# One order of VectorE's bit operations in the joint slots, and the start of eight weight conversions, changed in an attention and two-layer feed-forward kernel

## The chip, the cores and the metric

The kernel runs on one core of a Trainium2 chip. The metric is the device time of one execution in microseconds; the kernel before takes 620.14 us (median of 3 runs, 619.54 to 620.14).

Five engines work side by side and wait for each other by semaphores: TensorE (PE in the rows, with its weight loads as PEld), VectorE (DVE), ScalarE (ACT), GpSimd (POOL) and SyncE (SP), which only issues transfers here. Each runs its instructions in the order in which the program gave them.

## The reference

Attention over 2 x 8 heads of 768 positions and 64 channels with 8 global and 96 local positions, then two feed-forward layers on the 1536 x 512 result. All in float32; the weights arrive as float64 words.

```python
a = softmax(where(keep, scale * q @ k.T + bias, -1e9))
x = (a @ v).transpose(0, 2, 1, 3).reshape(1536, 512)
h = x @ moe_w_in                                  # 512 -> 2048
x = (maximum(h, 0) + alpha * minimum(h, 0)) @ moe_w_out
h = x @ moe2_w_in
g = P(h) / (Q(h) + 1e-6)                          # a rational function
return g @ moe2_w_out
```

## The kernel before, in words

**Tiling.** The attention goes by blocks of 128 queries; a pair of steps (two pairs of heads) is one `u`, from 0 to 23. The first layer of the feed-forward part goes by groups of 512 tokens and chunks of 128 hidden channels; one group and one chunk is one step. A step is a first product (line 859: 12 matmuls of 128 x 512 into one bank), the alpha unit on its result, and a second product (line 930: 12 matmuls). Every float32 operand of a product is split into a high half, rounded to the format in which TensorE reads, and a low half, the rest.

**Stages.** `u` 0 to 9 run alone (up to 42 us). Then come 16 joint slots, `joint_slot(s, halves)` (line 969), `s` 0 to 15, each of which runs `u = 10 + s` of the attention and step `s` of the first layer in one hand-written order. All later steps run in `plain_slot` (line 1004).

**One joint slot.** `opening(u)` (716): TensorE computes the scores of `u`, and in odd `u` the value products of two earlier `u`; VectorE takes the reciprocals of `u - 1` (563), after which GpSimd normalises (556), and adds the bias to the scores and takes the extreme (537, 4 instructions); ScalarE takes the exponentials (544, 4 instructions); in odd `u` ScalarE and VectorE store the two halves of a finished block (`xhi` 614, `xlo` 615). Then `first(s)`. `leaky(s)` (862) issues ScalarE's `act` (866) and VectorE's `h` (867); what it returns issues ScalarE's `ghi` (870), and what that returns VectorE's `glo` (871). `glo` is the last reader of bank 3, into which `first(s + 1)` writes. `turning(u)` (742): TensorE transposes the probabilities of `u - 1` (574, 576) into banks 0 and 1, where the bias instructions of `u` have read, and one block of raw keys (odd `u`) or queries (even `u`) into bank 2 (460); ScalarE copies the probabilities out (582) and takes the high halves of keys (475) or queries (489); the functions for the low halves (`klo` 479, `qlo` 490) are returned as `lows` for VectorE. `second(s - 1)` comes last.

**Weight conversions.** Half a chunk of weights (512 KB of float64 words) is one job. `tick` (353) is called twice in a slot, with numbers `2s - 1` and `2s`, and moves each started job on by one stage:

- at its start: ScalarE scales one word of the pair into one of two `de` buffers (397);
- one tick later: three VectorE bit operations that assemble the float32 (386, 387, 388; 386 and 387 read `de`, each reads the one before) and a call of `load_more` are put into the list `join`, from which `join_step(n)` issues up to `n`; the next load goes into the staging buffer that 388 has read;
- one tick later: the high half on ScalarE (372 where it is `held`, else 374), preceded by whatever is left in `join`;
- one tick later: the low half on VectorE (377).

Where a job starts at each tick there are two sets of bit operations in a slot: those of the job started at `2s - 3` (the older; issued whole inside the tick `2s - 1`) and those of the job started at `2s - 2` (the younger; issued by the `join_step` calls of `joint_slot`). The high half of the older is `held` until behind `ghi`; that of the younger, and the next scale, come with the tick `2s`.

**The plan.** `plan_weights` (253) gives each job the tick of its start. With `CH` = 8 and `KEPT` = 12, the jobs of the first eight chunks start at ticks up to 11; those of chunks 8 to 11, whose halves are written to DRAM (`spill`, 241) and read back later (`reload`, 246), at 10, 12, ..., 24; those of chunks 12 to 15 from 31 on. Transfers are issued by SyncE in program order.

Of the kernel before, what the change touches and what calls it, by code (L numbers as in the profile page):

```python
# [49 lines left out]
CH = NF // 2  # L50
KEPT = CH + 4
# [14 lines left out]
class Kernel:  # L66
# [186 lines left out]
    def plan_weights(self):  # L253
        self.steps = [(0, 0, fc, fc % NEARLY) for fc in range(CH)]
        self.steps += [(0, 1, fc, fc % NEARLY) for fc in (*range(NEARLY, CH), *range(NEARLY))]
        self.steps += [(0, 2, fc, fc) for fc in range(NF)]
        self.steps += [(0, g, fc, fc) for g in (0, 1) for fc in range(CH, NF)]
        self.steps += [(1, g, j, j) for g in (2, 0) for j in range(CH)]
        self.steps += [(1, 1, j, j) for j in range(NF)]
        self.steps += [(1, g, j, j) for g in (2, 0) for j in range(CH, NF)]  # L260
        runs = [s[:2] for s in self.steps]
        self.begins = {n for n in range(len(runs)) if n == 0 or runs[n - 1] != runs[n]}
        self.ends = {n - 1 for n in self.begins if n} | {len(runs) - 1}
        self.saves = {n for n in self.ends if runs[n] in runs[n + 1 :]}
        self.adds = {n for n in self.ends - self.saves if runs[n] in SAVED}
        jobs = {}
        for fc in range(CH):
            jobs[2 * fc - 6 if fc > 2 else 4 * fc - 17] = 0, fc, "in", fc % NEARLY
            jobs[2 * fc - 3 if fc else -5] = 0, fc, "out", fc % NEARLY
        half, layer = NGR * CH, NGR * NF  # L270
        spare = [(fc, kind) for fc in range(CH, NF) for kind in ("in", "out")]
        for t, (fc, kind) in enumerate(spare):
            jobs[10 + 2 * t if fc < KEPT else 15 + 2 * t] = 0, fc, kind, None if fc < KEPT else fc
        todo = []
        for n, free in ((0, LATE), (CH, layer - CH)):
            for k in range(CH):
                for kind, lag in (("in", 0), ("out", 5)):
                    todo.append((n + k, 2 * (free + k) + lag, kind))
        times = [t for t in range(48, 96) if (t % 2 == 0 or t in (55, 71) or t > 82) and t not in (64, 66, 80, 82, 85, 88, 91, 94, 95)]
        times += (107, 112, 117, 121, 125, *range(137, 160, 4))  # L280
        for t in times:
            ready = [x for x in todo if x[1] <= t]
            if ready:
                j, _, kind = job = min(ready)
                todo.remove(job)
                jobs[t] = 1, j, kind, j
        assert not todo
        self.starts = set(jobs)
        self.plan = [jobs[t] for t in sorted(jobs)]
# [555 lines left out]
    def moe(self):  # L845
# [6 lines left out]
        def first(n):  # L852
            m, g, fc, slot = steps[n]
            w = self.slots[slot]
            bk = banks[3 if n < LATE else n % 3]
            seq = [(a, b, c) for a, b in (("hi", "hi"), ("lo", "hi"), ("hi", "lo")) for c in range(NC)]
            for e, (a, b, c) in enumerate(seq):
                x = (self.xhi if b == "hi" else self.xlo)[g]
                nc.tensor.matmul(bk, w["in", a][:, c, :], x[:, c, :], start=e == 0, stop=e == len(seq) - 1)  # L859
            hbank[n] = bk  # L860

        def leaky(n):
            fc, h = steps[n][2], hbank.pop(n)
            t, hi, lo = self.act[n % 2], self.ghi[n % 2], self.glo[n % 2]
            sg, sa = self.sg[:, fc : fc + 1], self.sa[:, fc : fc + 1]
            nc.scalar.activation(t, h, AF.Copy, scale=sa)  # L866
            nc.vector.scalar_tensor_tensor(h, h, sg, t, ALU.mult, ALU.max)  # L867

            def halves():
                nc.scalar.activation(hi, h, AF.Copy, scale=sg)  # L870
                return lambda: nc.vector.scalar_tensor_tensor(lo, h, sg, hi.bitcast(F32), ALU.mult, ALU.subtract)  # L871

            return halves
# [43 lines left out]
        def second(n, parts=range(3)):  # L917
            m, g, fc, slot = steps[n]
            ys.add(n)
            w = self.slots[slot]  # L920
            hi, lo = self.ghi[n % 2], self.glo[n % 2]
            y = banks[4:8]
            begin, last = n in self.begins, n in self.ends
            wt = w["out", "hi"].rearrange("p c f -> p (c f)"), w["out", "lo"].rearrange("p c f -> p (c f)")
            order = [(d, e) for e in parts for d in range(4)]
            for d, e in sorted(order) if last else order:
                cols = slice(d * P, (d + 1) * P)
                a, b = ((hi, wt[0]), (hi, wt[1]), (lo, wt[0]))[e]
                lhs, rhs = (b[:, cols], a) if m == 0 else (a[:, cols], b)
                nc.tensor.matmul(y[d], lhs, rhs, start=begin and e == 0, stop=last and e == 2)  # L930
            if not last or 2 not in parts:
                return
            for d in range(4):
                if m == 0 or n == N - 1 or d < 3:
                    drain(n, d)
                else:
                    drains.append((n, d))
# [31 lines left out]
        def joint_slot(s, halves):  # L969
            u = JOIN // 2 + s  # L970
            opening, turning = halves or (lambda u: None, lambda u: ())
            if s >= CH + 2 and s < CH + 2 + NEARLY:
                self.reload(s - CH - 2)
            opening(u)
            held = []
            if s == 0:
                self.creep()
            else:
                while self.creeps:
                    self.creep()  # L980
                self.tick(True, 2 * s - 1 in self.starts, spread=True, held=held)
                self.join_step(2)
            first(s)
            halves = leaky(s)
            self.join_step(2)
            if s == 0:
                self.creep()
            lows = turning(u)
            low = halves()
            for high in held:  # L990
                high()
            for more in lows:
                more()
            low()
            if s == 0:
                self.creep()
            self.tick(True, 2 * s in self.starts, spread=True)
            if s:
                second(s - 1)
            if s == LATE - 1:  # L1000
                self.tick(True, 2 * s + 1 in self.starts)
                self.spill()
# [72 lines left out]
        def run(halves):  # L1075
            first_call = state["slot"] == 0
            if first_call:
                for s in range(LATE):
                    joint_slot(s, halves)
                state["slot"] = LATE  # L1080
                return
            self.moe_constants()
            for fc in range(NEARLY, CH):
                self.reload(fc)
            for s in range(LATE, N + 2):
                plain_slot(s)
# [41 lines left out]
```

## Time and profile before

| what | us |
|---|---|
| median of 3 runs | 620.14 (619.54 to 620.14) |
| the profiled execution | 619.92 |
| its span in the profile | 618.1 |
| TensorE busy, matmuls | 606.3 (98%) |
| VectorE busy | 498.4 (81%) |
| ScalarE busy | 404.7 (65%) |
| GpSimd busy | 130.8 (21%) |
| TensorE in the chain that ended last | 91% of the span |

The granted clock of TensorE is 0.9 or more of full speed in every one of the 40 slices of the page but the last. The joint slots lie between 42 and 174 us. In rows of instructions the columns are: start in us, duration in us, engine, line, operation, out<-in by the program's names, shapes and count; in square brackets the engine's idle time just before, and what ended it. Durations overlap a little with the next instruction on the same engine, so the step from one start to the next is the better price in a busy queue.

### The profile page before, as it was taken

Reading aid. Unit: us, or ns where it says so; the run is one execution under the profiler, and the core shown is the slowest. Engines: PE = TensorE matmul, PEld = TensorE weight load, DVE = VectorE, ACT = ScalarE, POOL = GpSimd, SP = SyncE. Lnnn points to the kernel's source line nnn. Section 1 sums busy time; section 2 is a strip of 40 time slices with the busy share of each in tenths; the row PEclk is TensorE's granted clock in tenths of the full one; section 3 lists DMA queues with packets and bytes.
Section 4 is the critical chain, followed back from the end, with each engine's and each line's share of the span. In section 5 each row is a group of like instructions: output and inputs, shape, how many; then the busy total and the mean of one; then the engine's idle time right before and its main releaser. Section 6 shows DMA issues by size and latency. Waiting matters only on the chain.

```text
span 618.1 us, 9432 instructions
## 1 busy us (share of the span) xinstructions
PE 606.3 (98%) x3187; PEld 499.1 (81%) x3187; DVE 498.4 (81%) x960; ACT 404.7 (65%) x826; POOL 130.8 (21%) x202
## 2 busy tenths in 40 slices
PE   8999999999999999999999999999999999999996
PEld 6688878888888888888888888888888888888884
DVE  6988899776457768668579889999899977788976
ACT  6997777876455444354354587787877766766772
POOL 6863223322100000000000012122222222222221
PEclk9999999999999999999999999999999999999998
DMA  9999999878889534315322401211201000400302
GB/s 211 252 277 272 284 291 299 289 261 271 251 275 353 169 97 116 95 35 150 123 68 70 135 1 34 89 47 37 101 1 35 0 1 0 137 1 1 136 1 74
DMA packets 81426, 82.53 MB, mean 134 GB/s; under 512 B 41994, under 2 KB 58394, under 8 KB 81370
## 3 DMA queue, kind: packets, MB, share of 16 engines
q1 hardware_dynamic: 81190, 81.58, 44.3%
q8 instruction: 27, 0.44, 0.3%
q14 instruction: 29, 0.24, 0.1%
q10 hardware_dynamic: 180, 0.27, 0.1%
HBM read 59.94 MB, written 19.92 MB: 129 GB/s over the span
## 4 chain that ended last, share of the span: by engine, by line
PE 91%; DVE 5%; ACT 2%; issue 1%; POOL 0%; DVEq 0%; ACTq 0%
PE bank L859 41%; PE bank L930 41%; PE bank L518 2%; PE bank L595 2%; PE bank L574 1%; PE bank L597 1%; ACT prob L544 1%; PE bank L576 1%; PE bank L460 1%; DVE prob L537 1%; DVE dx L388 1%; PE bank L201 1%; DVE dx L387 0%; DVE dx L386 0%; DVE glo L871 0%
## 5 line engine op out<-in xcount | busy, mean ns | idle before, releaser
L915 POOL TENSOR_TENSOR glo<-act,ghi 128x512 fp32r<-128x512 f32 (+1 forms) x49 | 62.4, 1274 | 382.8 <-ACT ghi L911 362.7
L859 PE MATMUL bank<-xhi,winhi_f 128*128 128x512 f32 x256 | 68.4, 389 | 0.0
L859 PE MATMUL bank<-xhi,winlo_f 128*128 128x512 f32 x256 | 68.4, 389 | 0.0
L859 PE MATMUL bank<-xlo,winhi_f 128*128 128x512 f32 x256 | 68.4, 389 | 0.0
L556 POOL TENSOR_SCALAR prob<-prob,rec 128x232 f32<-128x232 f32 (+1 forms) x96 | 48.8, 526 | 70.0 <-DVE rec L563 43.5
L867 DVE SCALAR_TENSOR_TENSOR bank<-bank,sg,act 128x512 f32<-128x512 f32 x48 | 36.3, 757 | 31.4 <-ACT act L866 31.3
L870 ACT ACTIVATE ghi<-bank,sg 128x512 fp32r<-128x512 f32 x48 | 33.3, 694 | 39.4 <-DVE bank L867 25.3
L866 ACT ACTIVATE act<-bank,sa 128x512 f32<-128x512 f32 x48 | 32.8, 683 | 37.6 <-PE bank L859 37.5
L859 PEld LDWEIGHTS bank<-xhi,winlo_f 128*128 128x128 f32 x256 | 48.0, 188 | 10.0
L859 PEld LDWEIGHTS bank<-xhi,winhi_f 128*128 128x128 f32 x256 | 48.0, 188 | 10.0
L859 PEld LDWEIGHTS bank<-xlo,winhi_f 128*128 128x128 f32 x256 | 48.0, 188 | 10.0
L544 ACT ACTIVATE prob<-prob,stat 128x232 f32<-128x232 f32 (+1 forms) x96 | 44.7, 470 | 14.9 <-DVE stat L537 12.8
L871 DVE SCALAR_TENSOR_TENSOR glo<-bank,sg,ghi 128x512 fp32r<-128x512 f32 x48 | 35.9, 747 | 18.8 <-PE bank L930 14.3
L882 ACT ACTIVATE stage<-bank 128x512 f32<-128x512 f32 (+1 forms) x49 | 28.8, 588 | 32.8 <-PE bank L859 32.8
L891 DVE SCALAR_TENSOR_TENSOR stage<-stage,abs_b 128x512 f32<-128x512 f32 (+1 forms) x49 | 36.1, 737 | 14.9 <-ACT stage L883 14.8
L397 ACT ACTIVATE de<-stage 128x512 f32<-128x512 f32 x59 | 39.5, 675 | 6.9 <-issue 3.2
L387 DVE SCALAR_TENSOR_TENSOR dx<-de,dx 128x512 int32<-128x512 int32 x59 | 40.9, 694 | 2.0
L388 DVE SCALAR_TENSOR_TENSOR dx<-stage,dx 128x512 int32<-128x512 int32 x59 | 40.9, 693 | 1.6
L911 ACT CAST ghi<-act 128x512 fp32r<-128x512 f32 (+1 forms) x49 | 30.2, 617 | 17.6 <-DVE act L908 15.2
L930 PE MATMUL bank<-wouthi_f,glo 128*128 128x512 f32 x144 | 41.1, 391 | 0.0
L930 PE MATMUL bank<-wouthi_f,ghi 128*128 128x512 f32 x144 | 40.9, 389 | 0.0
L930 PE MATMUL bank<-woutlo_f,ghi 128*128 128x512 f32 x144 | 40.9, 389 | 0.0
(240 smaller groups left out, 1418.4 us busy)
## 6 DMA issues: line engine op xcount, KB each, us to landing
stage<-in_moe_w_in_dram SPq DMA_DIRECT2D x32, 512.0 KB
stage<-in_moe_w_out_dram SPq DMA_DIRECT2D x32, 512.0 KB
part<-saved_f SPq DMA_DIRECT2D x16, 256.0 KB
saved_f<-part SPq DMA_DIRECT2D x12, 256.0 KB
out_dram<-part SPq DMA_DIRECT2D x11, 256.0 KB
rawk<-in_k_dram SPq DMA_DIRECT2D x10, 256.0 KB
rawq<-in_q_dram SPq DMA_DIRECT2D x10, 256.0 KB
va<-in_v_dram SPq DMA_DIRECT2D x10, 240.0 KB
```

Source lines behind the costliest of these rows:

```text
L387: lambda: nc.vector.scalar_tensor_tensor(y, e, -(2**31), y, ALU.bitwise_and, ALU.bitwise_or),
L388: lambda: nc.vector.scalar_tensor_tensor(y, low, 29, y, ALU.logical_shift_right, ALU.bitwise_or),
L397: nc.scalar.mul(self.de[n % 2], self.staged(n)[:, :, :, 1].bitcast(F32), 2.0**-112)
L544: nc.scalar.activation(p[:, j - e, :w], p[:, j - e, :w], AF.Exp, bias=st[:, j : j + 1], scale=-1.0, accum_out=st[:, 4 + j : 5 + j],)
L556: nc.gpsimd.tensor_scalar(p[:, j, :w], p[:, j, :w], r[:, e + j : e + j + 1], 1.0, ALU.mult, ALU.mult)
L859: nc.tensor.matmul(bk, w["in", a][:, c, :], x[:, c, :], start=e == 0, stop=e == len(seq) - 1)
L867: nc.vector.scalar_tensor_tensor(h, h, sg, t, ALU.mult, ALU.max)
L870: nc.scalar.activation(hi, h, AF.Copy, scale=sg)
L871: return lambda: nc.vector.scalar_tensor_tensor(lo, h, sg, hi.bitcast(F32), ALU.mult, ALU.subtract)
L891: nc.vector.scalar_tensor_tensor(w, w, self.ab[:, 0:1], ab, ALU.add, ALU.mult)
L915: nc.gpsimd.tensor_tensor(lo, u, hi.bitcast(F32), ALU.subtract)
L930: nc.tensor.matmul(y[d], lhs, rhs, start=begin and e == 0, stop=last and e == 2)
```

## The change

In `plan_weights`, the starts of the jobs of chunks 8 to 11 move four ticks on: 14, 16, ..., 28 instead of 10, 12, ..., 24. In `joint_slot`, slots 1 to 5 (`two`) issue no bit operation of the younger set ahead of `first` and `leaky`. In odd `u`, one of them follows `h`, then come `glo`, then `klo`, and `join_step(4)` issues the other two and `load_more`. In even `u` none follows `h`; `qlo` and `glo` come in the old order, then all three. In the other slots two bit operations still stand ahead of `h`; in odd `u` the third follows `h`, and `glo` comes ahead of `klo`; in even `u` the third follows `glo`.

```diff
         for t, (fc, kind) in enumerate(spare):
-            jobs[10 + 2 * t if fc < KEPT else 15 + 2 * t] = 0, fc, kind, None if fc < KEPT else fc
+            jobs[14 + 2 * t if fc < KEPT else 15 + 2 * t] = 0, fc, kind, None if fc < KEPT else fc
...
             opening(u)
             held = []
+            two = 0 < s < CH - 2
             if s == 0:
                 self.creep()
             else:
                 while self.creeps:
                     self.creep()
                 self.tick(True, 2 * s - 1 in self.starts, spread=True, held=held)
-                self.join_step(2)
+                self.join_step(0 if two else 2)
             first(s)
             halves = leaky(s)
-            self.join_step(2)
+            if u % 2:
+                self.join_step(1 if two else 2)
             if s == 0:
                 self.creep()
             lows = turning(u)
             low = halves()
             for high in held:
                 high()
-            for more in lows:
+            for more in (low, *lows) if u % 2 else (*lows, low):
                 more()
-            low()
+            self.join_step(4)
             if s == 0:
                 self.creep()
             self.tick(True, 2 * s in self.starts, spread=True)
```

## Rows read from the trace of the kernel before

**Rows 1.** Busy time by stretch: us, then each engine; clock, DMA share, GB/s.

```profile
67.20:92.50 25.30, 23.90 (x154) 19.22 (x152) 23.55 (x55) 19.44 (x51) 6.74 (x13) 1.00 0.99 283
...
110.00:176.00 66.00, 65.99 (x460) 54.48 (x459) 41.66 (x108) 41.32 (x103) 15.65 (x36) 1.00 0.86 276
```

**Rows 2.** Instructions in order of time, TensorE, slots 6 and 7.

```profile
92.51 1.19 PE L859 MATMUL bank<-xhi,winhi__120 128*128 128x512 f32 x4 [1.09 <-DVE glo L871]
...
96.19 0.60 PE L460 MATMUL bank<-part,rawq 128*128 128x128 f32 x4
...
102.11 1.19 PE L859 MATMUL bank<-xhi,winhi__124 128*128 128x512 f32 x4
```

**Rows 3.** Instructions in order of time, VectorE, slot 3.

```profile
67.95 0.69 DVE L615 TENSOR_TENSOR xlo<-bank,xhi 128x512 fp32r<-128x512 f32 x1 [1.48 <-ACT xhi L614]
...
69.61 0.69 DVE L387 SCALAR_TENSOR_TENSOR dx<-de,dx 128x512 int32<-128x512 int32 x1
70.34 0.69 DVE L388 SCALAR_TENSOR_TENSOR dx<-stage,dx 128x512 int32<-128x512 int32 x1
70.94 0.42 DVE L386 TENSOR_SCALAR dx<-de 128x512 int32<-128x512 int32 x1
71.40 0.69 DVE L387 SCALAR_TENSOR_TENSOR dx<-de,dx 128x512 int32<-128x512 int32 x1
72.01 0.75 DVE L867 SCALAR_TENSOR_TENSOR bank<-bank,sg,act 128x512 f32<-128x512 f32 x1
72.67 0.68 DVE L388 SCALAR_TENSOR_TENSOR dx<-stage,dx 128x512 int32<-128x512 int32 x1
73.27 0.75 DVE L479 TENSOR_TENSOR klo<-bank,khi 128x480 fp32r<-128x480 f32 x2
73.93 0.74 DVE L871 SCALAR_TENSOR_TENSOR glo<-bank,sg,ghi 128x512 fp32r<-128x512 f32 x1
74.59 0.69 DVE L377 TENSOR_TENSOR woutlo__127<-dx,wouthi__126 128x512 fp32r<-128x512 f32 x1
75.19 0.17 DVE L563 RECIPROCAL rec<-rec 128x4 f32<-128x4 f32 x1
```

**Rows 4.** The same for ScalarE, slot 3.

```profile
70.38 0.71 ACT L397 ACTIVATE de<-stage 128x512 f32<-128x512 f32 x1 [1.69 <-issue]
71.00 0.67 ACT L866 ACTIVATE act<-bank,sa 128x512 f32<-128x512 f32 x1
...
72.80 0.69 ACT L870 ACTIVATE ghi<-bank,sg 128x512 fp32r<-128x512 f32 x1
```

**Rows 5.** The same for VectorE, slot 2 and its ends.

```profile
57.72 0.29 DVE L537 CUSTOM_DVE_ANT_0 prob<-bank,part 128x128 f32<-128x128 f32 x1 [1.17 <-PE bank L518]
...
59.63 0.69 DVE L387 SCALAR_TENSOR_TENSOR dx<-de,dx 128x512 int32<-128x512 int32 x1
...
65.14 0.17 DVE L563 RECIPROCAL rec<-rec 128x4 f32<-128x4 f32 x1
```

**Rows 6.** The same for ScalarE, slot 2.

```profile
61.00 0.67 ACT L866 ACTIVATE act<-bank,sa 128x512 f32<-128x512 f32 x1
...
62.43 0.61 ACT L489 ACTIVATE qhi<-bank 128x512 fp32r<-128x512 f32 x1
```

**Rows 7.** The same for VectorE, the reciprocal at the start of slot 6.

```profile
92.96 0.17 DVE L563 RECIPROCAL rec<-rec 128x4 f32<-128x4 f32 x1
```

**Rows 8.** The same for GpSimd, the normalisations of slots 5 and 6.

```profile
83.94 1.76 POOL L556 TENSOR_SCALAR prob<-prob,rec 128x232 f32<-128x232 f32 x4 [4.05 <-DVE rec L563]
...
93.31 2.44 POOL L556 TENSOR_SCALAR prob<-prob,rec 128x232 f32<-128x232 f32 x4 [6.24 <-PE bank L859]
```

**Rows 9.** The chain that ended last, in order of time, a piece in the plain slots.

```profile
193.03 2.72 PE bank L859 x12
```

**Rows 10.** Instructions in order of time, VectorE, slot 4.

```profile
78.32 0.87 DVE L388 SCALAR_TENSOR_TENSOR dx<-stage,dx 128x512 int32<-128x512 int32 x1
```

**Rows 11.** The same for GpSimd, slot 4.

```profile
78.59 0.97 POOL L501 CAST klo<-klo 128x384 fp32r<-128x384 f32 x1
```

## What the trace gave reason to expect

> **What bounds the kernel now.** I read the stages first: busy time by stretch shows TensorE with 65.99 of 66.00 us from 110 to 176, and the plain slots behind that are as full; the only hole of any size after 42 us is 1.40 us of idle TensorE between 67.2 and 92.5, where VectorE is busy 23.55 of 25.30 us [rows 1]. So whatever TensorE loses in the joint slots is never won back, and whatever it gains there arrives whole at the end. Then the rows of TensorE: 1.09 us of the hole stand before one matmul, the first of slot 6, and their releaser is `glo` (line 871) on VectorE [rows 2]. Then VectorE instruction by instruction in slot 3 [rows 3], because a reordering is priced by what stands next to what; then ScalarE in the same slot [rows 4], because VectorE's line 867 (`h`) needs ScalarE's `act`, and `glo` needs ScalarE's `ghi`.
>
> What the reader should see in rows 3: from 69.61 to 75.19 each instruction starts as soon as the one before allows. A full bit operation takes a step of 0.60, or 0.73 if the next one reads its result; line 386 takes 0.46 before its reader; `h`, `klo` and `glo` 0.66 each; a low half (line 377) 0.60. In rows 4: the ScalarE scale of line 397 starts at 70.38, 0.08 after the older conversion's line 387 ends (69.61 + 0.69 = 70.30). It overwrites the `de` buffer that this instruction reads. `act` (line 866) is queued right behind it and ends at 71.67. VectorE comes to `h` at 72.01, so it doesn't wait: the younger conversion's lines 386 and 387 stand exactly in the time that ScalarE needs.
>
> **The change part by part.** *Order in slots 2 to 5 (two conversions).* Nothing is added or removed on VectorE; the younger's three bit operations move behind `glo` (one stays behind `h` in odd slots). Both directions must be counted: `glo` stands earlier in the queue, and the time in which ScalarE works is no longer filled.
>
> Take the start of the older's line 387 as zero. Scale at 0.77, `act` at 1.39 (step 0.62), `h` at 1.39 + 0.67 + 0.04 = 2.07 to 2.10 [rows 4]. VectorE is free at 0.73 + 0.60 = 1.33 [rows 3], so it now idles 0.75 us there; queued behind the waiting `h` is all the rest of the slot. `h` starts 0.3 us earlier than before (2.40).
>
> Odd slot: after `h` one short operation to 3.1; `ghi` starts 1.80 after `act` starts and takes 0.69, so `glo` can start only at 3.9: 0.8 us idle. Then `glo` 0.66, `klo` 0.66, the younger's remaining two operations 0.73 + 0.60 and the low half 0.60: the next slot's reciprocal at 7.15, against 5.58 before (69.61 to 75.19). Each such slot is **1.57 us longer** on VectorE [rows 3, 4].
>
> Even slot: `qlo` needs `qhi`, which ends 2.04 after `act` starts [rows 6], so it starts at about 3.45 with VectorE free at 2.73: 0.7 us idle. Then 0.60 + 0.66, the three bit operations 0.46 + 0.73 + 0.60 and the low half 0.60: 7.10, against 5.51 before (59.63 to 65.14 [rows 5]). **1.59 us longer**. In slot 4 the probability copies are half as wide; I estimate 1.3.
>
> *Slot 1* has only the younger set. By the same steps its end moves 1.9 us, but VectorE then idled 1.17 us for the scores [rows 5]: 0.7 is left.
>
> *Adding up the lateness of VectorE at the end of each slot.* Slot 1: 0.7. Slot 2: 0.7 + 1.6 = 2.3. Slot 3: before, VectorE idled 1.48 us for ScalarE's `xhi` until 67.95 [rows 3]. Now ScalarE's own queue is late too: the younger's high half waits for the last bit operation, and the scale, two exponentials and `xhi` stand behind it. Between 0 (the values on TensorE are in time) and the whole 2.3 I take 1.5, as some 2 us of ScalarE's instructions fill most of the 2.8 us between that reciprocal and `xlo` before. With 1.57 the end is 3.1 late. Slot 4: 4.4. Slot 5: 4.4 + 1.6 = 6.0, that is, the reciprocal of 92.96 [rows 7] at about 98.9.
>
> *What TensorE sees.* Up to the first matmul of slot 3 nothing: that one waits for `glo` of slot 2, which still ends before it. From slot 3 on, the reciprocal releases GpSimd's normalisation, that releases the transposes, and the bias passes behind the reciprocal free the banks that these write; so TensorE waits at the transposes, and once more at the scores and at `glo`. The delay is read where the last of these ends, in slot 6. The normalisation starts 0.35 after the reciprocal and takes 2.44 in this place (93.31), 1.76 one slot earlier (83.94) [rows 8]. The input transposes then start about 0.2 behind its end, at 98.9 + 0.35 + 1.76 to 2.44 + 0.2 = 101.2 to 101.9. From there to the first matmul of slot 7 TensorE's own work was 102.11 - 96.19 = 5.92 [rows 2], which gives 107.1 to 107.8 against 102.11: **5.0 to 5.7 us late**. I take 5.5, nearer the upper end, because 2.44 is the row for this very place.
>
> *Where the stall ends.* Slot 6 now has one conversion where it had two (the second part of the change), so its VectorE end comes near 106.9 and the normalisation for slot 7 is done by 109 to 109.7; the first product of slot 7 (2.72 for twelve matmuls [rows 9], from 107.6) ends at 110.3. From there TensorE is the bound again. Without the second part VectorE would end slot 6 near 108.6 and the transposes would wait once more, 0.4 to 1.1.
>
> *Spilled chunks four ticks on.* Eight conversions are the same work later; slots 6 and 7 lose one set of bit operations, scale and both halves each, and slots 14 and 15 gain one. There VectorE is idle most of the time: in 110 to 176 it is busy 41.66 of 66.00 [rows 1]; cost nothing, cover TensorE. The transfers move too: two loads of 512 KB and four spills of 256 KB, 2 MB, pass from before 110 to after. At the 276 GB/s of that stretch this is 7.6 us of transfer time, and the stretch has 14% of 66 = 9.2 us free [rows 1]. On SyncE's queue the last spill now waits for a low half that VectorE reaches only at the end of slot 15 (about 175 on the old clock, an estimate from where rows 1 end the stage), and the reloads of chunks 4 to 7 are queued behind it. Their first reader is the product at 193.03 [rows 9], so some 17 us remain. Zero, with a bound of +3 if a reload then needs 20 us.
>
> *Other slots.* With one conversion, even slots place line 388 behind `glo`, odd slots place `glo` ahead of `klo`. From slot 8 VectorE has the slack of rows 1: zero, -0.1 to +0.1.
>
> *GpSimd beside VectorE.* In slot 4 line 388 took 0.87 instead of 0.69 [rows 10, 3] while line 501 copied keys on GpSimd (0.97) [rows 11]. The lag moves these copies against other VectorE work: 0 to +0.5, which the sum holds half of. The Trainium skill (SBUF — State Buffer, Who interferes with whom) says of the port pair that VectorE and GpSimd share that the second to issue fully blocks until the first finishes. By that rule alone the two copies could add up to twice 0.97, some 1.9 us, for 627.5; the row shows 0.18 on one instruction, which is not a full block.
>
> **Sum.** The profiled execution took 619.92 us (618.1 of span, 1.8 around it), 0.22 below the median of 620.14. 619.92 + 5.5 = 625.4; against the median, 625.6.
>
> **The rivals.**
>
> *Faster.* If `act` were ready when VectorE comes to `h`, the move would cost nothing, `glo` would be 1.7 us earlier, and all of the 1.40 us hole could go: 618.7. For it: the hole is there and `glo` is its releaser. Against: it needs the scale on ScalarE to start 0.75 us earlier than the older's line 387 lets it, and it started 0.08 behind that line [rows 3, 4]. 10%.
>
> *Half the loss.* If the scale is released by something earlier than line 387 (the trace names no releaser for it), the first idle of 0.75 falls away in four slots and only that at `glo` or `qlo` stays: 5.5 - 3.0 = 2.5, 622.6. 12%.
>
> *More loss.* Reloads late (+3) or longer blocks between GpSimd and VectorE (+1.9): 627.5 to 628.6. 8%.
>
> *No change.* The idle times all fall into waits that VectorE had anyway, as 1.17 and 1.48 us in slots 1 and 3 did [rows 3, 5]; in slots 4 and 5 there is next to none: 4%.
>
> **How the numbers follow.** Forecast 66%, with 624 to 627 as its own range (slot increments 0.2 either way, normalisation 1.76 to 2.44, port 0 to 0.5). A measurement of this kernel tells 0.2%, 1.2 us, from no change. Slower by more: 66 + 12 + 8 = 86%; within: 4%; faster by more: 10%. The range 622.3 to 628 takes in the half loss and most of the larger one and leaves out the faster case, the unchanged one and the end of the larger, about 16%.
>
> **What would show it.** Right: in slots 2 to 5 VectorE idles about 0.7 us before line 867 with ScalarE's `act` as releaser, and again before `glo` (odd) or `qlo` (even); the reciprocals fall behind by 2 to 6 us; TensorE waits at the transposes (line 574) for GpSimd or VectorE in slots 4 to 6; from slot 7 the gap between the two traces stays constant, and after 176 us TensorE is full. Wrong: line 867 starts without idle time, or the reciprocal near 92.96 comes at 95 or sooner, or TensorE waits after 185 us for a reload.

## The result, and the profile after

The changed kernel takes **624.88 us** (median of 6 runs, 624.50 to 625.99), the kernel before 620.12 in the same comparison: ratio 1.0085, 95% interval 1.0075 to 1.0095. It is slower by 4.8 us; the forecast was 625.6. The span of its profiled execution is 622.8 us, against 618.1.

Read the stages first. Busy time by stretch in the changed kernel; columns as in [rows 1]:

```profile
42.00:67.20 25.20, 24.70 (x192) 20.14 (x190) 20.68 (x56) 18.38 (x50) 8.88 (x18) 1.00 1.02 271
67.20:97.20 30.00, 26.67 (x163) 20.61 (x160) 24.39 (x64) 19.92 (x55) 8.09 (x17) 1.00 0.97 266
97.20:115.00 17.80, 16.41 (x124) 13.10 (x122) 14.18 (x38) 12.58 (x33) 5.43 (x10) 1.00 0.93 251
115.00:181.00 66.00, 66.00 (x459) 54.48 (x460) 44.57 (x114) 43.68 (x106) 15.35 (x34) 1.00 0.67 212
181.00:350.00 169.00, 169.00 (x747) 139.96 (x746) 123.77 (x198) 83.01 (x138) 0.49 (x2) 1.00 0.50 166
```

TensorE's hole of 1.40 us in [rows 1] has become 3.33 us in the second stretch and 1.39 us in the third. From 115 to 350 us there is none. Between the first matmuls of the same product in the two traces the distance is 5.00 us at slot 7, 4.90 at slot 8 and 4.89 at every later step, and 4.7 at the end of the span: nothing more is lost, and next to nothing is won back. VectorE is idle for 5.6 of 30 us in the second stretch, where it was idle for 1.75 of 25.3.

Then VectorE in slot 3, instruction by instruction, to be laid beside [rows 3]:

```profile
69.17 0.69 DVE L615 TENSOR_TENSOR xlo<-bank,xhi 128x512 fp32r<-128x512 f32 x1 [0.99 <-ACT xhi L614]
...
70.83 0.69 DVE L387 SCALAR_TENSOR_TENSOR dx<-de,dx 128x512 int32<-128x512 int32 x1
71.56 0.69 DVE L388 SCALAR_TENSOR_TENSOR dx<-stage,dx 128x512 int32<-128x512 int32 x1
72.90 0.76 DVE L867 SCALAR_TENSOR_TENSOR bank<-bank,sg,act 128x512 f32<-128x512 f32 x1 [0.65 <-ACT act L866]
73.57 0.42 DVE L386 TENSOR_SCALAR dx<-de 128x512 int32<-128x512 int32 x1
74.57 0.75 DVE L871 SCALAR_TENSOR_TENSOR glo<-bank,sg,ghi 128x512 fp32r<-128x512 f32 x1 [0.58 <-ACT ghi L870]
75.23 0.74 DVE L479 TENSOR_TENSOR klo<-bank,khi 128x480 fp32r<-128x480 f32 x2
...
77.82 0.17 DVE L563 RECIPROCAL rec<-rec 128x4 f32<-128x4 f32 x1
```

VectorE now stands idle before `h` (867) until ScalarE's `act` is there, and before `glo` until `ghi` is; in [rows 3] it waited for neither. From the older set's line 387 to the next reciprocal it is 6.99 us, against 5.58. The two waits, and `qlo` in even slots, grouped over slots 0 to 5 (42 to 97 us; count, busy us, mean ns, then idle us before them and its releaser):

```profile
L867 DVE SCALAR_TENSOR_TENSOR bank<-bank,sg,act 128x512 f32<-128x512 f32 x6 | 4.6, 759 | 3.9 <-ACT act L866 3.9
L871 DVE SCALAR_TENSOR_TENSOR glo<-bank,sg,ghi 128x512 fp32r<-128x512 f32 x6 | 4.5, 747 | 2.5 <-ACT ghi L870 2.5
L490 DVE SCALAR_TENSOR_TENSOR qlo<-bank,qhi 128x512 fp32r<-128x512 f32 x3 | 2.1, 692 | 0.9 <-ACT qhi L489 0.9
```

That is 7.3 us of idle time; in the kernel before the same three groups had 0.6, all before `h`. ScalarE in the same slot, beside [rows 4]:

```profile
71.61 0.68 ACT L397 ACTIVATE de<-stage 128x512 f32<-128x512 f32 x1 [1.69 <-issue]
72.18 0.69 ACT L866 ACTIVATE act<-bank,sa 128x512 f32<-128x512 f32 x1
```

The scale (397) starts 0.09 after the older set's line 387 ends (70.83 + 0.69 = 71.52), as it did before by 0.08; the profile again names no releaser for it ("issue"), though ScalarE had stood still for 1.69 us.

Last, where TensorE waits (67.2 to 115 us, grouped by line and tile), and the start of slots 6 and 7 beside [rows 2]:

```profile
L574 PE MATMUL bank<-part,prob 128*128 128x128 f32 x20 | 4.4, 285 | 2.8 <-POOL prob L556 2.1 <-DVE stat L537 0.7
L460 PE MATMUL bank<-part,rawk 128*128 128x128 f32 x12 | 1.9, 278 | 0.3 <-DVE xlo L615 0.3
L859 PE MATMUL bank<-xhi,winhi__112 128*128 128x512 f32 x5 | 1.7, 436 | 0.6 <-DVE glo L871 0.6
L859 PE MATMUL bank<-xhi,winhi__120 128*128 128x512 f32 x4 | 1.2, 420 | 1.0 <-DVE glo L871 1.0
```

```profile
95.67 1.20 PE L859 MATMUL bank<-xhi,winhi__120 128*128 128x512 f32 x4 [0.99 <-DVE glo L871]
...
99.37 0.30 PE L574 MATMUL bank<-part,prob 128*128 128x128 f32 x1 [0.69 <-POOL prob L556]
...
101.22 0.60 PE L460 MATMUL bank<-part,rawq 128*128 128x128 f32 x4
...
107.11 1.20 PE L859 MATMUL bank<-xhi,winhi__124 128*128 128x512 f32 x4
```

The transposes (574) wait for GpSimd's normalisation, which the late reciprocal holds up, and the first product of slot 6 still waits for `glo`.

Where the time went, by slots: each figure is the distance from one slot's first matmul of line 859 to the next slot's, from the rows of TensorE in order of time.

| slot | 0 | 1 | 2 | 3 | 4 | 5 | 6 | 7 | 0 to 7 |
|---|---|---|---|---|---|---|---|---|---|
| before | 7.70 | 7.81 | 9.57 | 7.54 | 8.78 | 9.00 | 9.60 | 7.91 | 67.91 |
| after | 7.69 | 7.81 | 10.08 | 8.11 | 10.36 | 9.94 | 11.44 | 7.81 | 73.24 |

The joint slots lost 5.33 us. In this execution slot 0 began at 41.68 us instead of 42.11, which hides 0.43 of it in absolute times; in the profiled executions of before, after, e1, e2, e5, e7 and e9 (below), whose programs don't differ up to there, that start lies between 41.68 and 42.36. The table counts from slot 0 for this reason. Counted so, the two traces are 5.1 us apart at the end of the span; the medians are 4.8 apart, and no row places the 0.3 between them. Rows of TensorE show 3.6 us more idle time between 42 and 115 us; the remaining 1.7 lies in groups counted as busy, mostly the scores (line 518, 14.5 against 13.7 us) and the transposes (574, 7.5 against 6.8), whose matmuls overlap less where they are released one by one.

### The profile page after: what moved, and what is told of

Its sections match the earlier page's. It is cut to its first block, busy times and chain, and to the rows that moved or that the text cites. A ratio compares the mean times of both kernels' runs of the same rounds, so it can differ in the third digit from the quotient of the medians.

```text
span 622.8 us, 9423 instructions
## 1 busy us (share of the span) xinstructions
PE 608.1 (98%) x3187; PEld 498.8 (80%) x3187; DVE 499.6 (80%) x960; ACT 404.9 (65%) x826; POOL 132.5 (21%) x202
## 4 chain that ended last, share of the span: by engine, by line
PE 83%; DVE 2%; ACT 2%; issue 1%; POOL 0%; POOLq 0%; ACTq 0%
PE bank L930 40%; PE bank L859 39%; PE bank L518 1%; PE bank L595 1%; PE bank L574 1%; PE bank L597 1%; PE bank L576 0%; POOL prob L556 0%; DVE prob L537 0%; PE bank L460 0%; ACT prob L544 0%; ACT de L397 0%; DVE dx L387 0%; ACT pt L582 0%; ACT act L866 0%
```

## The experiments

Each was timed beside the kernel before on the same chip (619.42 us with e1 to e4, 619.65 with e5 to e8, 619.38 with e9 and e10; 620.12 with the change). The idle time is the sum of the three groups above (before `h`, `glo`, `qlo`, 42 to 97 us).

| kernel | us | ratio, 95% interval | over before, us | idle, us |
|---|---|---|---|---|
| before | | 1 | 0 | 0.6 |
| changed | 624.88 | 1.0085 [1.0075, 1.0095] | +4.8 | 7.3 |
| e1 order alone | 626.32 | 1.0110 [1.0094, 1.0125] | +6.9 | 7.0 |
| e2 starts alone | 619.19 | 0.9997 [0.9988, 1.0006] | -0.2 | |
| e3 changed, third `de` buffer | 621.91 | 1.0047 [1.0033, 1.0060] | +2.5 | 4.4 |
| e4 changed, two operations ahead | 621.32 | 1.0030 [1.0019, 1.0042] | +1.9 | 3.8 |
| e5 changed in slot 3 alone | 621.25 | 1.0028 [1.0017, 1.0038] | +1.6 | 3.3 |
| e6 low halves on GpSimd | 622.88 | 1.0056 [1.0043, 1.0070] | +3.2 | |
| e7 `glo` ahead of `klo` alone | 620.42 | 1.0013 [1.0004, 1.0022] | +0.8 | 1.8 |
| e8 third buffer in before | 619.36 | 0.9998 [0.9989, 1.0007] | -0.3 | |
| e9 as e6, queued behind | 620.72 | 1.0022 [1.0013, 1.0032] | +1.3 | |
| e10 as e8, 15 jobs | 619.54 | 1.0004 [0.9995, 1.0013] | +0.2 | 0.5 |

### The two parts apart: e1 and e2

e1 keeps the new order and has the old starts; e2 the reverse.

```diff
-            jobs[14 + 2 * t if fc < KEPT else 15 + 2 * t] = 0, fc, kind, None if fc < KEPT else fc
+            jobs[10 + 2 * t if fc < KEPT else 15 + 2 * t] = 0, fc, kind, None if fc < KEPT else fc
```

> The new order with the old starts of the eight spilled conversions. Theory A (the loss is VectorE's empty time before line 867 and before line 871 or 490): the whole loss is there, and slot 6 with two sets adds 0.3 to 1.0 to the 624.9 of the change: 625.2 to 625.9. Theory B (the loss comes from the moved conversions and their transfers): near 620.

> The old order with the eight spilled conversions four ticks on. Theory A: 619.8 to 620.4, no change, since the only hole of TensorE stands before slot 6 and the sets taken away are in slots 6 and 7. Theory B: 623 or more, with TensorE waiting for a reload or SyncE after 160 us.

e2 came out at no change, as expected: the late starts neither cost nor bring anything by themselves, and in the changed kernel no reload is late (TensorE is full from 181 to 350 us in the first fence above). e1 was slower than the change by 2.1 us, each taken against the kernel before on its chip, where 0.3 to 1.0 was expected, which is outside. The spans of the profiled executions differ by 1.8 (624.6 and 622.8), and rows account for it: 0.68 is the start of slot 0 (42.36 against 41.68), 0.34 lies in slots 0 to 6 (65.77 against 65.43 from slot 0 to slot 7), 0.26 in slot 7 (8.07 against 7.81), and 0.51 is idle time of TensorE behind it:

```profile
116.20 1.20 PE L859 MATMUL bank<-xhi,winhi__112 128*128 128x512 f32 x4 [0.19 <-DVE glo L871]
120.16 0.33 PE L574 MATMUL bank<-part,prob 128*128 128x128 f32 x1 [0.32 <-POOL prob L556]
```

These two rows are e1's TensorE in slot 8. So what the second set in slots 6 and 7 costs is 0.77 us (0.26 + 0.51) by the rows, which is inside the expected bounds. The 0.34 arises earlier, in VectorE's slot 4: beside GpSimd, line 386 took 0.60 us and line 387 0.87 there, against 0.42 and 0.69 in the changed kernel, and the slot took 9.52 us from reciprocal to reciprocal (78.48 to 88.00) against 9.15. The 0.68 stands before anything that differs. Counted from slot 0 the two traces are thus 1.1 us apart; the rest of the 2.1 is not shown by any row.

### Which wait carries the loss: e3 and e4

e3 is the changed kernel with a third buffer for the scaled words, for the first 16 jobs, so that the scale (397) no longer overwrites what the older set's line 387 reads.

```diff
+    def de_of(self, n):
+        return (*self.de, self.third)[n % 3] if n < 16 else self.de[n % 2]
...
-            nc.scalar.mul(self.de[n % 2], self.staged(n)[:, :, :, 1].bitcast(F32), 2.0**-112)
+            nc.scalar.mul(self.de_of(n), self.staged(n)[:, :, :, 1].bitcast(F32), 2.0**-112)
```

> The change, with a third buffer for the scaled words in the joint slots, so that the scale on ScalarE (line 397) need not wait for the older conversion's line 387. Theory A: act is ready earlier, the idle time before line 867 in slots 2 to 5 (0.46 to 0.65 us each) goes, that before glo or qlo stays or shrinks: 621.5 to 623. Theory C (the scale is released by something else, or the idle time there is not what costs): 624.5 to 625.2, with the scale still 0.08 us behind line 387 or without effect on the end.

Half of the loss is gone. ScalarE and VectorE in slot 3 of e3 (400 is the scale, 389 is 386, 390 is 387, 391 is 388, 872 is `h`, 876 is `glo`):

```profile
69.64 0.68 ACT L400 ACTIVATE de<-stage 128x512 f32<-128x512 f32 x1
```

```profile
70.66 0.69 DVE L390 SCALAR_TENSOR_TENSOR dx<-de,dx 128x512 int32<-128x512 int32 x1
71.38 0.69 DVE L391 SCALAR_TENSOR_TENSOR dx<-stage,dx 128x512 int32<-128x512 int32 x1
71.99 0.75 DVE L872 SCALAR_TENSOR_TENSOR bank<-bank,sg,act 128x512 f32<-128x512 f32 x1
72.66 0.41 DVE L389 TENSOR_SCALAR dx<-de 128x512 int32<-128x512 int32 x1
73.50 0.75 DVE L876 SCALAR_TENSOR_TENSOR glo<-bank,sg,ghi 128x512 fp32r<-128x512 f32 x1 [0.43 <-ACT ghi L875]
```

The scale now starts 1.02 us before the older set's second bit operation (70.66) and not 0.09 behind its end. `h` follows without a gap, in slots 4 and 5 too (in slot 2 it still waits 0.26); the wait for `ghi` stays. So the releaser of the scale that the profile doesn't name is the read of the `de` buffer by line 387.

e4 is the changed kernel with two of the younger's operations ahead of `h` again, and the third behind `glo`.

```diff
-                self.join_step(0 if two else 2)
+                self.join_step(2)
             first(s)
             halves = leaky(s)
             if u % 2:
-                self.join_step(1 if two else 2)
+                self.join_step(0 if two else 2)
```

> The change, but in slots 1 to 5 two bit operations of the younger set stand ahead of line 867 again, and only the third follows glo. Theory A: line 867 has no idle time before it and a third operation behind glo costs little: 620.0 to 621.0. Theory D (what costs is that the set ends later, so the high half on ScalarE and all behind it come late): the third operation still ends behind glo, so a good part of the loss stays: 622 to 624.

`h` waits no more in slots 2 to 5, but 621.32 lies 0.3 above the expected end, and about 1 above it when this chip's 619.42 for the kernel before is taken into account. I had kept the wait before `glo` at that of the change, but with nothing between `h` and `glo` in odd slots it grows: 0.76 us in slot 3 against 0.58, and 3.1 against 2.5 over slots 0 to 5. Theory D has no clear row: behind the late high half stands ScalarE's `xhi`, and VectorE waits no longer for it than in the kernel before (2.6 against 2.8 us over three odd slots). So rows show the direction of the miss, but not all of its 1 us.

```profile
71.65 0.75 DVE L867 SCALAR_TENSOR_TENSOR bank<-bank,sg,act 128x512 f32<-128x512 f32 x1
73.15 0.75 DVE L871 SCALAR_TENSOR_TENSOR glo<-bank,sg,ghi 128x512 fp32r<-128x512 f32 x1 [0.76 <-ACT ghi L870]
```

### One slot, and one edit: e5 and e7

e5 applies the new placement of the younger set in slot 3 alone. The other slots of e5 are not those of the kernel before: `glo` stands ahead of `klo` in odd slots, the third operation behind `glo` in even ones, and the starts are late. e7 is the kernel before with nothing but `glo` ahead of `klo` in odd slots.

```diff
-            two = 0 < s < CH - 2
+            two = s == 3
```

```diff
-            for more in lows:
+            for more in (low, *lows) if u % 2 else (*lows, low):
                 more()
-            low()
```

> The changed kernel, with the younger conversion's operations behind glo in slot 3 alone; slots 1, 2, 4 and 5 put two of them ahead of h and one behind it or behind glo, close to the old order. Theory A (ScalarE's time for the scale, act and ghi is left unfilled, 1.5 to 1.6 us of VectorE in a slot, and nothing behind slot 3 gives it back before TensorE waits): 1.2 to 1.8 over the kernel before, 620.6 to 621.3. Rival B (the loss arises only where several slots add up past a slack of some 2 us): within 0.4 of the kernel before. Rival C (only the idle time at glo counts): 0.6 to 0.8 over it.

> The kernel before, with one part of the change alone: in odd slots glo stands ahead of klo; the younger's operations stay in their old places and no start is moved. Theory A (the younger's move is the cost; this order costs 0.3 us of waiting for ghi in slots 3 and 5 and lets glo come 0.3 to 0.6 sooner, where slot 6 waits for it): 0.5 faster to 0.4 slower than the kernel before, 618.9 to 619.8. Rival B (the loss came from glo ahead of klo): at least 2 slower, 621.4 or more.

e5 gives 1.6 us, as much as was worked out for one slot, but that agreement is in part chance, since not all of it comes from slot 3. In slot 3 the same two waits stand as in the changed kernel (0.66 before `h`, 0.58 before `glo`), and the reciprocal behind it comes at 76.61, 1.42 later than before. Slot 4 adds 0.26 (85.28, 1.68 late) and slot 5, where `glo` waits 0.35, adds 0.45 (95.10, 2.13 late). In e7 slot 5 adds 0.43 too. Counted from slot 0 as in the table of slots, TensorE in e5 loses 1.87 us in slots 0 to 7, so most of VectorE's lateness arrives: a slack of some 2 us is excluded. Against e7, which shares the order of `glo` and `klo`, e5 costs 0.8 us more. e7 is 0.8 slower than the kernel before, 0.4 more than I had allowed: `glo` stands before its `ghi` in every odd slot (1.2 us of idle time over three slots), and what it gains for slot 6 is 0.3 of the 1.09 us. It excludes the rival that this edit is the main cost.

### Is the third buffer a gain of its own: e8 and e10

Both are the kernel before with the buffer of e3.

> The kernel before with a third buffer for the scaled words (de), so that the scale of line 397 doesn't wait for the older set's line 387. Theory A (before, the younger's two operations fill that time, so there is nothing to win): within 0.3 of the kernel before, and what the third buffer gave the changed kernel (2.4) is time that the change had lost. Rival B (a third buffer helps any order): 1 to 2.4 faster, 617.0 to 618.4.

> The kernel before with the third buffer for the scaled words, as e8, but in use for the first 15 conversions instead of 16, so that no two conversions in a row share a buffer. Theory A (before, the younger's two operations fill the time in which ScalarE works, so there is nothing to win): within 0.3 of the kernel before. Rival B (a third buffer helps any order): 1 to 2.4 faster.

In e8 jobs 15 and 16 share a buffer at successive ticks, so one conversion reads words that the next has already replaced, and its half chunk of weights comes out wrong; the instructions are the same. e10 has no such pair. Both take the time of the kernel before, so the 2.3 us that the buffer gave the changed kernel is time that the change had lost.

### A use for GpSimd: e6 and e9

If 0.60 us of VectorE in a slot is worth 0.60 us of TensorE, three low halves moved to GpSimd, which is idle for 4 to 6 us at a time there ([rows 8]), should win back the hole. They are the older set's, which end slots 3 to 5, and not the younger's as the expectation below has it.

```diff
+LOWS = (6, 8, 10)
...
-            self.splits.append(lambda: nc.vector.tensor_sub(lo, x, hi.bitcast(F32)))
+            on_pool = self.ticks in LOWS
+            self.splits.append(
+                (lambda: nc.gpsimd.tensor_tensor(lo, x, hi.bitcast(F32), ALU.subtract))
+                if on_pool
+                else (lambda: nc.vector.tensor_sub(lo, x, hi.bitcast(F32)))
+            )
```

> The kernel before, with three of the younger set's low halves (line 377, those popped at ticks 6, 8 and 10, that is at the ends of slots 3 to 5) on GpSimd instead of VectorE; order and starts are the old ones. Theory A (each instruction taken off VectorE in these slots is 0.60 us off the way to the next reciprocal, and TensorE's 1.40 us of idle time is all there is to win): 0.6 to 1.2 faster than the kernel before, 618.2 to 618.8. Rival B (the GpSimd subtraction stands ahead of the normalisation on GpSimd's queue, or stretches VectorE beside it, by as much as it saves): between 0.3 faster and 1.5 slower.

Slower by 3.2, outside both expectations. GpSimd in slots 3 and 4 of e6 (380 is the moved low half, 568 the sum that the reciprocal reads, line 562 before), and the reciprocal on VectorE (569):

```profile
73.72 1.28 POOL L380 TENSOR_TENSOR woutlo__127<-dx,wouthi__126 128x512 fp32r<-128x512 f32 x1 [7.18 <-DVE klo L485]
75.09 0.19 POOL L568 TENSOR_SCALAR rec<-stat 128x4 f32<-128x4 f32 x1
```

```profile
75.32 0.18 DVE L569 RECIPROCAL rec<-rec 128x4 f32<-128x4 f32 x1 [1.00 <-POOL rec L568]
84.89 0.18 DVE L569 RECIPROCAL rec<-rec 128x4 f32<-128x4 f32 x1 [1.96 <-POOL rec L568]
```

GpSimd's 7.18 us of idle time were not free: the sum used to run at 68.85 in the middle of them, and now stands behind a subtraction whose high half ScalarE ends at 73.63 (the profile names `klo`, which ends at 73.66; for the next subtraction, in slot 4, it names that high half). I had counted idle time and not looked at what is queued. e9 puts the subtraction behind the normalisation of the next slot.

```diff
+                self.behind.append(
+                    lambda: (
+                        nc.gpsimd.tensor_tensor(lo, x, hi.bitcast(F32), ALU.subtract),
...
             both_ready(u - 1)
+            while self.behind:
+                self.behind.pop()()
```

> As e6, with the same three low halves on GpSimd, but queued behind GpSimd's normalisation of the next slot instead of ahead of the sum that the reciprocal reads (line 562 of the kernel before); the low half is spilled one tick later. Theory A (in e6 the loss was the sum standing behind a subtraction that waited for ScalarE's high half; with the queue free each reciprocal comes 0.6 sooner per slot, and the 1.1 us that TensorE waits for glo ahead of slot 6 goes): 0.3 to 1.1 faster than the kernel before, 618.5 to 619.4. Rival B (the subtraction itself, 1.28 us beside VectorE, or the next set's line 386 that must wait for it, takes back what the three halves give): from the same time to 1.5 slower.

Now the reciprocal of slot 4 comes 0.63 sooner (74.56), but the kernel is 1.3 us slower: rival B. GpSimd and VectorE of e9 beside it (388 is the low half on VectorE, 398 and 400 the first and last bit operation, 383 the subtraction on GpSimd):

```profile
76.28 1.72 POOL L383 TENSOR_TENSOR woutlo__127<-dx,wouthi__126 128x512 fp32r<-128x512 f32 x1
...
85.67 1.29 POOL L383 TENSOR_TENSOR woutlo__115<-dx,wouthi__114 128x512 fp32r<-128x512 f32 x1
...
95.62 1.71 POOL L383 TENSOR_TENSOR woutlo__119<-dx,wouthi__118 128x512 fp32r<-128x512 f32 x1
```

```profile
75.95 0.90 DVE L388 TENSOR_TENSOR winlo__117<-dx,winhi__116 128x512 fp32r<-128x512 f32 x1
76.78 1.51 DVE L398 TENSOR_SCALAR dx<-de 128x512 int32<-128x512 int32 x1
...
86.32 1.19 DVE L388 TENSOR_TENSOR winlo__121<-dx,winhi__120 128x512 fp32r<-128x512 f32 x1
...
96.23 1.66 DVE L400 SCALAR_TENSOR_TENSOR dx<-stage,dx 128x512 int32<-128x512 int32 x1
```

In slot 4 the first bit operation took 1.51 us instead of 0.42, in slot 5 the low half 1.19 instead of 0.69, and in slot 6 the last bit operation 1.66 instead of 0.69. Each subtraction moved away saves VectorE 0.60 us, and the three cost it 1.09, 0.50 and 0.97 beside them. No version here is faster than the kernel before beyond the noise.

## Why the prediction came out as it did

**The mechanism** held in its main steps. `h` waits in slots 2 to 5 with `act` as releaser, `glo` waits in odd slots and `qlo` in even ones, the transposes wait for GpSimd, the gap is constant from slot 7 on to 0.1 us, and TensorE is full behind it. e1 and e2 put the cost in the order, e3 and e4 show its two halves, and e7 and e10 exclude its neighbours as the main cause. Two statements failed, that TensorE loses nothing in slot 2 and that GpSimd doesn't block VectorE fully; neither changed the sum by much.

**VectorE's lateness at the end of each slot** (reciprocals, line 563), beside what was predicted; the last column counts from slot 0, that is, adds the 0.43 us by which this execution began it sooner:

| reciprocal | before | after | late | predicted | late from slot 0 |
|---|---|---|---|---|---|
| start of slot 3 | 65.14 | 67.19 | 2.05 | 2.3 | 2.48 |
| start of slot 4 | 75.19 | 77.82 | 2.63 | 3.1 | 3.06 |
| start of slot 5 | 83.60 | 86.97 | 3.37 | 4.4 | 3.80 |
| start of slot 6 | 92.96 | 98.12 | 5.16 | 6.0 | 5.59 |

- *Odd slots*, predicted 1.57 from line 387 to the reciprocal: slot 3 took 1.41 more (6.99 against 5.58), slot 5 took 1.76 more (90.78 to 98.12, 7.34). In slot 5 `glo` waited 0.93 instead of 0.58.
- *Slot 4* is the term that was mis-sized: 1.3, an estimate, against 0.74 from reciprocal to reciprocal (9.15 against 8.41). I had scaled it for the narrower probability copies, but the row for it was [rows 10, 11]: before, GpSimd's copies of keys (line 501) stretched two VectorE instructions, 388 to 0.87 and 386 behind it to 0.73; after, only 388 is stretched (0.87), and both this and the rest of the second copy fall into the time in which VectorE waits for `act` anyway. So some 0.5 us of the slot before was interference that the new idle time took in. Line 386 in the kernel before, then 388 in the changed one:

```profile
79.12 0.73 DVE L386 TENSOR_SCALAR dx<-de 128x512 int32<-128x512 int32 x1
```

```profile
80.95 0.87 DVE L388 SCALAR_TENSOR_TENSOR dx<-stage,dx 128x512 int32<-128x512 int32 x1
```

- *Slot 3's xlo*: I took 1.5 us of lateness out of a range of 0 to 2.3, it was 1.22 (69.17 against 67.95).
- *Slot 2*, from which I expected TensorE to lose nothing, lost 0.51: one of its transposes waited 0.30 for the normalisation. It is hidden in the start of slot 3 (67.26 against 67.19), because slot 0 began 0.43 sooner.
- *The last link*: reciprocal at 98.12, normalisation 98.46 with 2.44 us, input transposes at 101.22 (predicted 101.2 to 101.9), from there 5.89 to the first product of slot 7 (taken as 5.92). So 107.11, 5.00 late, 5.43 counted from slot 0; I had taken 5.5 from 5.0 to 5.7. That it comes so near is in part chance: VectorE was 0.41 less late than summed (5.59 against 6.0), and from the reciprocal to the input transposes it took 3.10 us, above the 2.31 to 2.99 that I had added.

**The shift of the starts** was rightly put at zero in itself (e2). Its worth once the order is changed, 0.4 to 1.1, is 0.77 by the rows of e1. The whole kernels differ by more (2.1), and of that the rows show only 0.34 more, a collision with GpSimd in slot 4.

**The rivals.** *Half the loss* fell by the rows: the scale again starts 0.09 behind line 387, and e3 shows that this wait is the other half (2.3 of 4.8; the prediction had 3.0 of 5.5). *Faster* had the same condition, and e3 shows that the condition would not have been enough: with `act` ready in slots 3 to 5 the kernel is still 2.5 us slower, since the wait for `ghi` stays. *More loss* by late reloads: no row. *More loss* between GpSimd and VectorE: in the changed kernel the copies and normalisations stretched single instructions by 0.19 at most (a low half in slot 2, 0.88 instead of 0.69), which is inside the 0 to 0.5 of the sum. The prediction's reason for it was wrong all the same, as the last section shows.

Idle time of VectorE and time lost go together over most kernels in the table of the experiments. Beyond the 0.6 us of the kernel before, 1.2 us of idle time cost 0.8 (e7), 2.7 cost 1.6 (e5), 3.2 cost 1.9 (e4), 3.8 cost 2.5 (e3) and 6.7 cost 4.8 (the change): 0.6 to 0.7 us per us. e1 doesn't lie on this line (6.4 us cost 6.9); it also has a second set in slots 6 and 7. Part of the idle time falls in slots 0 and 1, where VectorE had waits of its own ([rows 5], 1.17).

## What to carry to other kernels

On an in-order engine, price a reorder by what it leaves empty: lay the other engine's chain (here scale, `act`, `ghi`) beside the queue, count from the instruction that releases it, and see which work stood in that time. A start that the profile puts down to "issue" after a long idle time may be held by a buffer that another engine still reads; look for the instruction that ends 0.1 us before it, and give it one more buffer to test that. And idle time of an engine is only free if nothing with an earlier reader is queued behind what you put there.

## What the runs showed of the hardware

VectorE and GpSimd held each other up in turn, and how much depended on what was left of the instruction that had started first. Slot 4 of the kernel before, beside [rows 10, 11]:

```profile
77.66 0.98 POOL L501 CAST khi<-khi 128x384 fp32r<-128x384 f32 x1
```

Line 388 started at 78.32, with 0.32 us of this copy left, and took 0.87 us instead of 0.69: it ended 0.55 us after the copy (79.19 against 78.64). Line 386 started at 79.12, with 0.44 us of the second copy left, and took 0.73 instead of 0.42: it ended 0.29 us after that copy (79.85 against 79.56). Beside GpSimd's two-input subtraction in e9 the distances are the same: 0.29 us for the first bit operation (76.28 + 1.72 = 78.00), 0.55 for the low half (85.67 + 1.29 = 86.96) and 0.56 for the last bit operation (95.62 + 1.71 = 97.33). Each is 0.13 to 0.14 us less than the instruction takes alone, as if it had begun only when GpSimd's ended. That is what the Trainium skill (SBUF — State Buffer, Who interferes with whom) says, that the second to issue fully blocks until the first finishes. The prediction had set this rule aside because line 388 lost only 0.18 us, but only 0.32 us of the copy were left when it started.

GpSimd waited likewise. The same copy took 0.51 us in e6, where VectorE stood idle, and 0.97 beside VectorE in the kernel before:

```profile
84.06 0.51 POOL L507 CAST klo<-klo 128x384 fp32r<-128x384 f32 x1
```

The subtraction took 1.28 us in e6 (73.72), where VectorE ran only the end of `glo`, and 1.72 in e9, where a VectorE low half with two inputs (75.95 to 76.85) was running when it began at 76.28.

Not every row is so simple. In slot 6 of the kernel before, line 386 started at 95.09 while GpSimd's normalisations lasted to 95.75 (93.31 + 2.44), and took its usual 0.41 us; which engine goes first when both are waiting isn't shown here.
